# A delta-rule attention followed by an MLP mixer: elements 2 and 3 in one joint recurrence, their mixers in groups of 384 tokens with 15 block products for both channel products

## The chip, the cores and the metric

The kernel runs on one core of one Trainium2 chip. The metric is the device time of one execution in microseconds (us). Before the change it is 638.55 us, the median of three runs that lie between 637.54 and 639.22 us. The profile shown below is one further execution of the same program, and its span, from the first to the last instruction, is 636.9 us; the change is reckoned against that span, and the 1.6 us between it and the median are added at the end.

## The reference

Two blocks follow each other. The first is a delta-rule attention over batch 4, 8 heads, 768 tokens, head width 48; the second is an MLP mixer over the result, laid out as 4 elements of 768 tokens by 384 channels.

```python
k_n = k / (np.linalg.norm(k, axis=-1, keepdims=True) + 1e-06)
for t in range(S):
    y[:, :, t] = np.einsum('bhd,bhde->bhe', q[:, :, t], state)
    v_old = np.einsum('bhde,bhd->bhe', state, kt)
    state = state + bt[:, :, :, None] * np.einsum('bhd,bhe->bhde', kt, vt - v_old)
...
x = attn_out.transpose(0, 2, 1, 3).reshape(B, S, H * D)
xt = x.transpose(0, 2, 1)
h = np.maximum(xt @ w_tok1, 0.0) @ w_tok2
u = x + h.transpose(0, 2, 1)
h2 = np.maximum(u @ w_ch1, 0.0) @ w_ch2
return u + h2
```

The token product goes from 768 tokens to 256 and back, the channel product from 384 channels to 1536 and back. Everything is float32.

## The kernel before

The kernel is one stream of some 4,650 TensorE matmuls, with the other engines around them. All its parts are Python generators, called jobs. A long string, `order`, names the jobs one after the other (`m1*5` advances job m1 five times), and each advance issues the instructions up to the next `yield`. Every engine executes its own instructions strictly in the order in which that string issued them, and semaphores hold it where its data are not ready. So the string fixes the order on each engine, and not the time at which one engine passes another. A matmul of float32 stands twice in the trace, as two records; a transpose on TensorE stands once.

The recurrence is cut into chunks of 64 tokens, 12 for each batch element, 48 in all. Two chunks are a unit u of 128 tokens. For a unit, `load_kq`, `prep` and `grams` load keys and queries, norm them, turn them and form the Gram matrices; `to_parts`, `invert`, `from_parts` and `join` invert a triangular matrix for the unit (by way of DRAM from the second element on: n_dram, w_dram). `load_v` brings the values, and GpSimd scales them (L426).

`recur(t)` then makes one chunk of one element for its 8 heads, in three groups of small matmuls with a hand-over between each two: p_k from the state (L862); VectorE subtracts the values into rest (L869); p_y and p_w (L882, L886); ScalarE copies p_w into w_t (L892); p_s and p_y (L900, L901); VectorE brings the state up to date (L909), and ScalarE puts p_y into xb, the element's 768x384 block (L914). The four elements follow each other: element 3 begins when element 2 is through.

`mixer(b)` is the MLP for one element, and TensorE works on it between the groups of the recurrence of the next element; the last one, m3, has TensorE almost to itself. It is:

- the token products: 12 matmuls of 128x384 (L1060), a ReLU, 12 more (L1073) and six additions into xb on VectorE (L1077);
- then three pairs of 128-token blocks. Each pair is transposed (L1083, evicted by ScalarE at L1087), goes through the first channel product and then through the second;
- the first channel product of element 0 is plain: 36 matmuls with 256 columns (L1140). From element 1 on (`FAST = 1`) it goes by `wide_fast`: a bilinear scheme that makes a 3 by 3 by 2 block product, 18 block products when done plainly, with 15. Its weight blocks are summed once, in place over wc1, by `sum_weights` (VectorE, L973); its 11 sums of input blocks are made for every pair by `forms` (VectorE, L1001, 128x128 each). Each of the 15 products is 4 matmuls with 128 columns (L1032), evicted from PSUM by ScalarE copies (L1041) or VectorE additions (L1044) of 512 columns, with a ReLU at the end (L1048);
- the second channel product goes by a 2 by 2 scheme with 7 products instead of 8 (`product`, L1162): 42 matmuls with 192 columns for a pair, seven additions into xb (L1091), and a store.

The weights come in by `round_weights` and `round_pair`; the latter also makes the sums of w_ch2 blocks for the 7-product scheme (L299). PSUM has eight banks: two each under the tags prep and seq, three under mlp, one for filler matmuls.

What the chunks of the chain look like in the code before:

## Time and profile before

| | |
|---|---|
| device time, median of 3 runs (lowest to highest) | 638.55 us (637.54 to 639.22) |
| span of the profiled execution | 636.9 us |
| TensorE (PE) busy | 608.5 us, 96% of the span |
| VectorE (DVE) busy | 447.9 us, 70% |
| ScalarE (ACT) busy | 268.0 us, 42% |
| GpSimd (POOL) busy | 107.2 us, 17% |
| weight loads on TensorE (PEld), over and under the matmuls | 531.5 us, 83% |
| granted TensorE clock, mean | 0.976 of full speed |
| data moved by DMA | 50.27 MB, mean 79 GB/s |

How to read the profile: a row of the groups by line says line, engine, operation, the tiles written and read, shapes and count, then busy time in us, mean duration of one in ns, and idle time of the engine before them with what ended it. Matmuls are pipelined, so that the duration of one record (some 200 to 500 ns) is longer than the distance at which records follow each other; a price per matmul is taken from start to start. A row of the chain of waits says start, length and what ran; a row of the timeline says start, length and instruction, with equal neighbours merged.

### The profile page before, as it was taken

What the parts mean: (1) busy time and instruction counts of PE and PEld (TensorE: products, weight loads), DVE (VectorE), ACT (ScalarE), POOL (GpSimd) and SP (SyncE); (2) the same over time, 40 slices, a digit from 0 to 9 for tenths busy, and PEclk for the clock granted to TensorE, in tenths of its full rate; (3) what the DMA queues carried; (4) which work ended last, traced back from release to release, by engine and by line L of the source; (5) the groups of instructions that cost most, each with busy time, mean ns of one, the idle gap of its engine ahead of it and who ended that gap; (6) DMA issues with size and microseconds to landing.
All of it is one profiled execution on the core that took longest, in us unless ns stands there. A gap on an engine that the chain in (4) does not pass through costs nothing.

```text
span 636.9 us, 21542 instructions
## 1 busy us (share of the span) xinstructions
PE 608.5 (96%) x9132; PEld 531.5 (83%) x9132; DVE 447.9 (70%) x1132; ACT 268.0 (42%) x693; POOL 107.2 (17%) x146
## 2 busy tenths in 40 slices
PE   8488988899999999999999999999999999999997
PEld 5367877668898988859889999769999987999997
DVE  4987876967999658988969987776728253373643
ACT  7758785447523342215624323325334130232240
POOL 2348354235210211111111001000010000000000
PEclk9978796999999999999999999999999999999999
DMA  9686666666543355344454223202020000000000
GB/s 201 127 148 151 153 142 153 162 135 162 110 113 89 71 116 101 76 109 79 90 103 95 43 82 58 48 5 42 5 53 2 27 2 0 26 1 26 2 26 26
DMA packets 135776, 50.27 MB, mean 79 GB/s; under 512 B 114656, under 2 KB 130144, under 8 KB 135680
## 3 DMA queue, kind: packets, MB, share of 16 engines
q1 hardware_dynamic: 135680, 48.89, 35.2%
q8 instruction: 72, 1.18, 0.8%
q14 instruction: 24, 0.20, 0.1%
HBM read 39.42 MB, written 9.44 MB: 77 GB/s over the span
## 4 chain that ended last, share of the span: by engine, by line
PE 82%; DVE 7%; ACT 4%; DMA 3%; issue 2%; POOL 1%; SPq 1%; ACTq 0%; DVEq 0%; POOLq 0%
PE p_o L1162 26%; PE p_r L1032 20%; PE p_c L1140 8%; PE p_h L1073 5%; PE p L1060 4%; PE p_k L862 3%; PE p_g L453 3%; PE p_y L882 3%; PE p_s L900 3%; PE p_w L886 1%; DVE sub L681 1%; DVE x L686 1%; PE p_y L901 1%; PE p_ut L1083 1%; PE p_z L785 1%
## 5 line engine op out<-in xcount | busy, mean ns | idle before, releaser
L1162 PE MATMUL p_o<-wc,r 128*128 128x192 f32 x720 | 126.1, 329 | 0.6 <-ACT u_t L1087 0.6
L1162 PEld LDWEIGHTS p_o<-wc,r 128*128 128x128 f32 x720 | 116.8, 190 | 2.7 <-ACT u_t L1087 1.1
L1044 DVE TENSOR_TENSOR r<-r,p_r 128x512 f32<-128x512 f32 x90 | 59.8, 684 | 38.1 <-PE p_r L1032 34.3
L1091 DVE TENSOR_TENSOR xb<-xb,p_o 128x192 f32<-128x192 f32 x84 | 29.3, 350 | 57.8 <-PE p_o L1162 57.3
L1041 ACT COPY r<-p_r 128x512 f32<-128x512 f32 x54 | 31.3, 585 | 85.7 <-PE p_r L1032 76.1
L686 DVE TENSOR_TENSOR x<-x,sub 128x84 f32<-128x84 f32 (+24 forms) x178 | 59.4, 334 | 6.1
L681 DVE TENSOR_TENSOR sub<-x 128x84 f32<-128x84 f32 (+24 forms) x178 | 58.0, 326 | 6.8 <-DMA x<-n_dram 2.3
L1162 PE MATMUL p_o<-wc,s 128*128 128x192 f32 x288 | 51.5, 331 | 0.3 <-DVE xb L1091 0.3
L1140 PE MATMUL p_c<-u_t,wc 128*128 128x256 f32 x216 | 51.0, 386 | 0.2 <-ACT u_t L1087 0.2
L1162 PEld LDWEIGHTS p_o<-wc,s 128*128 128x128 f32 x288 | 46.7, 190 | 1.4 <-DVE xb L1091 0.6
L1048 ACT ACTIVATE r<-r 128x512 f32<-128x512 f32 x54 | 34.0, 631 | 26.7 <-DVE r L1044 26.2
L426 POOL TENSOR_TENSOR v_st<-v_st,nrm 128x384 f32<-128x384 f32 x24 | 20.1, 838 | 146.3 <-DMA v_st<-in_v_dram 109.3
L1140 PEld LDWEIGHTS p_c<-u_t,wc 128*128 128x128 f32 x216 | 39.7, 190 | 6.0 <-ACT u_t L1087 0.4
L516 POOL TENSOR_TENSOR mb<-mask_c,cs 128x512 f32<-128x512 f32 x20 | 21.2, 1062 | 138.9 <-DVE cs L494 138.6
L914 ACT ACTIVATE xb<-p_y 64x192 f32<-64x192 f32 x96 | 31.2, 325 | 23.6 <-PE p_y L901 12.2
L892 ACT COPY w_t<-p_w 128x192 f32<-128x192 f32 x48 | 15.2, 316 | 58.0 <-PE p_w L886 57.5
L1032 PE MATMUL p_r<-u_t,wc 128*128 128x128 f32 x288 | 38.7, 277 | 0.0
L453 PE MATMUL p_g<-kq 48*64 48x128 f32 (+1 forms) x704 | 33.6, 281 | 3.8 <-ACT kq L529 3.3
L1032 PE MATMUL p_r<-t_d,wc 128*128 128x128 f32 x288 | 37.3, 280 | 0.0
L1032 PEld LDWEIGHTS p_r<-u_t,wc 128*128 128x128 f32 x288 | 35.3, 192 | 0.4
L1060 PE MATMUL p<-xb,w 128*128 128x384 f32 x96 | 34.9, 511 | 0.0
L1032 PEld LDWEIGHTS p_r<-t_d,wc 128*128 128x128 f32 x288 | 34.0, 192 | 0.8
(184 smaller groups left out, 1212.2 us busy)
## 6 DMA issues: line engine op xcount, KB each, us to landing
d<-in_moe_w_ch_dram SPq DMA_DIRECT2D x24, 384.0 KB, 3.5
v_st<-in_v_dram SPq DMA_DIRECT2D x96, 48.0 KB, 2.7
out_dram<-xb SPq DMA_DIRECT2D x23, 192.0 KB, 1.9
kst<-in_k_dram SPq DMA_DIRECT2D x64, 48.0 KB, 2.9
n_dram<-gm SPq DMA_DIRECT2D x72, 32.0 KB, 2.4
pads<-in_k_dram SPq DMA_DIRECT2D x24, 96.0 KB, 2.9
pads<-in_q_dram SPq DMA_DIRECT2D x24, 96.0 KB, 2.9
gm<-w_dram SPq DMA_DIRECT2D x72, 32.0 KB, 2.1
```

The source lines that it names most:

```text
L453: nc.tensor.matmul(p_g[PAR[i ^ cc], p], kqt[f, p, cc, 0], kqt[f, p, cc])
L681: nc.vector.tensor_tensor(out=tmp, in0=y[:, :, 0:s, s : s + 1].to_broadcast([n, k, s, w]), in1=y[:, :, s : s + 1, s + 1 : m].to_broadcast( ...
L686: nc.vector.tensor_tensor(out=y[:, :, 0:s, s + 1 : m], in0=y[:, :, 0:s, s + 1 : m], in1=tmp, op=ALU.add,)
L914: nc.scalar.mul(y[:, :, D * i : D * i + D], p_y[PAR[1 - i]], 1.0 if c else -1.0)
L1032: nc.tensor.matmul(p[:, i], pieces[i // width][:, at : at + 128], f[f"u{n}"], start=first and i == 0, stop=True, skip_group_check=True,)
L1041: nc.scalar.copy(o, p)
L1044: nc.vector.tensor_tensor(out=o, in0=o, in1=p, op=ALU.add if sign > 0 else ALU.subtract)
L1048: nc.scalar.activation(o, o, ACTF.Relu)
L1060: nc.tensor.matmul(p_1[dh], piece_of(w1, c, 0)[:, dh * 128 : (dh + 1) * 128], xb[:, c], start=(c == 0), stop=(c == NCH - 1),)
L1073: nc.tensor.matmul(p_h, piece_of(w2, j, c * 128)[:, c * 128 : (c + 1) * 128], r1[j], start=(j == 0), stop=(j == NDH - 1),)
L1140: nc.tensor.matmul(p_c[:, k], piece_of(wc1, cb, f * 128)[:, f * 128 : (f + 1) * 128], u_t[:, cb], start=(cb == 0), stop=(cb == NCB - 1),)
L1162: nc.tensor.matmul(p, a[:, m], wc2[:, m, j], start=(start and i == 0), stop=(i == NM - 1), skip_group_check=True,)
```

## The change

It does four things.

1. Elements 0 and 1 keep their recurrences. Elements 2 and 3 run in one joint recurrence, `recur_pair(c)`: 12 steps, each with 16 heads (8 of each element) in the same three groups, and with one operation of 384 columns where two of 192 stood. Units 12 to 23 alternate between the two elements (`where`). Element 2's output goes into its xb; element 3's goes into a corner of the pads tile and from there to DRAM (x_dram), because both xb buffers are still in use, and `fetch_last` loads it back.
2. The mixer of element 1 takes the plain first channel product (as element 0's), and the second by 7 products as before.
3. The mixers of elements 2 and 3 are written anew, in four groups of 384 tokens (g = 0 to 3). `token_part` is the old token product. `first_part(g)` is the first channel product by 15 of 18 block products, 2 halves of 15 steps, each step two matmuls with 192 columns. `act_forms(g)` sums blocks of its result on GpSimd, 15 additions of 128x512. `last_part(g)` is the second channel product by the same 15-product scheme with the two operands' roles exchanged, 15 steps of four matmuls with 192 columns, each evicted by VectorE additions of 192 columns. The sums of w_ch2 blocks for it are made late, by `tail_weights` on VectorE; since the blocks that `round_pair` overwrites are needed for that, `put_aside` copies one of them for each m to DRAM (wc_dram) beforehand.
4. The string `order` is new from the first inversion (i0) on; before that it is the same.

```diff
-    nrms = tiles("nrm", [128, NP, 2], NV + 2)
+    nrm_t = const.tile([128, NV + 2, NP, 2], FP32, name="nrm")
...
-    FAST = 1
...
+    def put_aside(m):
+        assert (id(wc2), 2 * m) in rounded
+        nc.sync.dma_start(out=wc_dram[m], in_=wc2[:, m, 1])
+        put_by.add(m)
+        yield
...
+    def recur_pair(c):
...
+        heads = [
+            (e, p, i, PAR[i ^ cc], PAR[1 - i])
+            for e in range(2) for p in range(NP) for i in range(2)
+        ]
+        rest = rw_t
+        if c > 0:
+            p_k = ps_seq([128, 2, NP, D], "p_k")
+            for n, (e, p, i, r, _) in enumerate(heads):
+                f = FEATS[i]
+                nc.tensor.matmul(p_k[r, e, p], ops[e][1][f, p, cc, 0], ss_t[f, e, p])
...
+            nc.vector.tensor_tensor(out=rest, in0=p_k, in1=vsts["pair", c], op=ALU.subtract)
...
+        nc.scalar.copy(rw_t, p_w)
...
+                nc.vector.tensor_tensor(out=ss_t, in0=ss_t, in1=p_s, op=ALU.subtract)
...
+        nc.sync.dma_start(
+            out=x_dram[C * c : C * c + C].rearrange("s (i n) -> s i n", i=2),
+            in_=side[rows],
+        )
...
+    r2_of = [
+        t[:, 0:RT].rearrange("p (f n) -> p f n", f=NHT) for t in (gm_flat, kq_flat)
+    ]
...
+    def tail_weights():
+        nc.sync.dma_start(out=wc2[:, :, 1], in_=wc_dram.rearrange("m p n -> p m n"))
+        yield
+        for out, x, y, sign in SUMS_3:
+            x, y = (w_of[z] if isinstance(z, str) else wc_blocks[z] for z in (x, y))
+            nc.vector.tensor_tensor(out=w_of[out], in0=x, in1=y, op=op_of(sign))
+            yield
+        nc.vector.tensor_scalar_mul(w_of["u7"], w_of["u7"], -1.0)
+        yield
...
+    def first_part(g):
...
+        f = named(bl, late(9, [128, 4, TW], 4))
+        for n, (out, x, y, sign) in enumerate(SUMS_3):
+            x, y = (f[z] if isinstance(z, str) else bl[z] for z in (x, y))
+            nc.vector.tensor_tensor(out=f[out], in0=x, in1=y, op=op_of(sign))
+            if n % 2 == 1 or n == 10:
+                yield
+        for half in range(2):
...
+            for chain, n, reads in CHAINS:
+                first = chain not in bank
+                if first:
+                    bank[chain] = ps_mlp([128, 2, TW], "p_r")
+                p = bank[chain]
...
+                for i in range(2):
+                    q = 2 * half + i
+                    at = q % width * 128
+                    nc.tensor.matmul(
+                        p[:, i], pieces[q // width][:, at : at + 128], f[f"u{n}"],
+                        start=first and i == 0, stop=True, skip_group_check=True,
+                    )
+                yield
+                for j, e, sign, last in reads:
+                    at = FT * j + 2 * half
+                    o = r2[:, at : at + 2, TW * e : TW * e + TW]
+                    if (j, e) not in begun:
+                        nc.scalar.copy(o, p)
...
+                    else:
+                        nc.vector.tensor_tensor(out=o, in0=o, in1=p, op=op_of(sign))
+                    if last:
+                        nc.scalar.activation(o, o, ACTF.Relu)
...
+    def act_forms(g):
...
+        for out, x, y, sign in (
+            ("w12", (1, 2), (0, 2), -1), ("w3", (1, 0), (0, 0), -1),
+            ("w1", (0, 0), (1, 2), -1), ("w5", (1, 2), (2, 0), 1),
...
+        ):
+            x, y = (f[z] if isinstance(z, str) else a[z] for z in (x, y))
+            nc.gpsimd.tensor_tensor(out=f[out], in0=x, in1=y, op=op_of(sign))
+            yield
...
+    def last_part(g):
...
+            for i in range(FT):
+                nc.tensor.matmul(
+                    p, a[:, i], w[:, i // 2, i % 2],
+                    start=first and i == 0, stop=True, skip_group_check=True,
+                )
+            yield
+            for j, e, sign, last in reads:
+                cut = slice(DH * e, DH * e + DH)
+                o = xb[:, c0 + j, cut]
+                nc.vector.tensor_tensor(out=o, in0=o, in1=p, op=op_of(sign))
...
+    j23*3 r34*3 T2*2 v23*4 s r34*7 v23 m1*2 r35*4 T2 r35*3 T2
+    r33 r35*6 s*7 T2 s T2*4 A0*7 T2*3 A0*16 s*2 A0*41 l*6 A0*5 A1 T3*3 F0*4 B0 A1
+    W*11 T3*3 W*2 B0 A1*3 B0 F0*2 T3*3 B0*2 A1*20 F0*2 B0*2 F0*3 B0 A1*4 B0 F0
+    A1*24 B0*2 A1*2 B0 A1*2 B0 A1*4 B0*3 A1*8 A2 B0 A2 B0*4 T3*3 A2 B0*2 F1 A2*8
+    F0 A2*4 B0*3 A2*3 F0*2 A2*6 F1*9 B0 F1*5 B0 A2*2 B0 A2*5 B1 A2*22 B1*10 A2*4
+    B1*3 A2*3 B0 A2 B1*2 A2*4 F2 A2*4 B1*6 A3*9 B1*3 F2 B1*2 A3*8 F2*5 B2 A3*4 B2
+    A3*3 B1*2 A3*3 B2*2 A3*4 B2*3 F2*4 B2 F2*2 B2*2 F2*2 A3*22 B1 B2*3 A3*5 B2*2
+    A3*5 B2*4 A3*4 F3 A3*2 F3*4 B2*9 B3*5 F3*5 B2*2 B3*13 F3*4 B3 F3 B3*11
```

In the string, r is a step of the recurrence (r24 to r35 are the joint ones), m0 and m1 the mixers of elements 0 and 1, T2 and T3 `token_part`, A, F and B `first_part`, `act_forms` and `last_part` of a group, W `tail_weights`, s `sum_weights`, l `fetch_last`.

More of the change, by code (lines that the diff above doesn't have):

```diff
@@ L1176, in mixer @@
             if c + 2 < NCH:
-                u_t, t_c = yield from turn_pair(c + 2)
+                u_t = yield from turn_pair(c + 2)
             yield from product(p_o2, a12, 2, True)
@@ L1220 @@
         jobs[f"i{rnd}"] = invert(rnd)
-    for t in range(B * NQ):
+    for t in range(B * NQ // 2):
         jobs[f"r{t}"] = recur(t)
-    for b in range(B):
+        if t < NQ:
+            jobs[f"r{B * NQ // 2 + t}"] = recur_pair(t)
+    jobs["l"] = fetch_last()
+    for b in range(2):
         jobs[f"m{b}"] = mixer(b)
+        jobs[f"T{2 + b}"] = token_part(2 + b)
+    jobs["W"] = tail_weights()
+    for g in range(4):
+        jobs[f"A{g}"] = first_part(g)
+        jobs[f"F{g}"] = act_forms(g)
+        jobs[f"B{g}"] = last_part(g)
     pieces = [
@@ L1233 @@
         jobs[f"w{j}"] = piece
+    for m in range(NM):
+        jobs[f"q{m}"] = put_aside(m)
     jobs["s"] = sum_weights()
```

494 lines of the change are left out of this document (332 added, 162 removed), and 23 rows, old and new, of tables (CHAINS, SUMS_3, bank, w4).

## The prediction

> **What bounds the kernel now.** I read the page's engine shares and its chain of waits first, then the sums by stretches of time, then the chain in order of time for prices, then the groups by line and the timelines of single places.
>
> ```profile
> span 636.9 us, 21542 instructions
> PE 608.5 (96%) x9132; PEld 531.5 (83%) x9132; DVE 447.9 (70%) x1132; ACT 268.0 (42%) x693; POOL 107.2 (17%) x146
> ...
> PE 82%; DVE 7%; ACT 4%; DMA 3%; issue 2%; POOL 1%; SPq 1%; ACTq 0%; DVEq 0%; POOLq 0%
> ```
>
> ```profile
> 0.00:150.00 150.00, 127.52 (x2568) 98.55 (x2568) 114.46 (x302) 102.43 (x276) 62.40 (x84) 0.90 0.72 153
> 150.00:550.00 400.00, 397.95 (x5953) 351.57 (x5954) 288.82 (x729) 142.20 (x379) 44.78 (x63) 1.00 0.30 65
> 550.00:600.00 50.00, 49.41 (x374) 48.42 (x373) 30.18 (x74) 16.09 (x28) 0.00 (x0) 1.00 0.04 13
> 600.00:637.00 37.00, 33.67 (x242) 32.98 (x240) 14.42 (x29) 7.30 (x12) 0.00 (x0) 1.00 0.06 22
> ```
>
> In the second view the columns are the stretch, its length, the busy time of PE, PEld, DVE, ACT and POOL with counts, the granted clock, the DMA share and GB/s. TensorE sets the end. It idles 22.5 us in the first 150, where loads and the inversion hold it (clock 0.90), and 2.05 us in the next 400. So a matmul saved after 150 us is worth its distance to the next one, and a stall there adds in full. POOL does nothing after 550 us.
>
> **Matmul work.** The prices of the dense matmuls stand in the chain in order of time (start, length, what; two records make one matmul):
>
> ```profile
> 194.81 9.26 PE p_c L1140 x42
> ...
> 519.01 7.74 PE p L1060 x24
> ...
> 577.44 13.67 PE p_r L1032 x120
> ...
> 594.01 12.07 PE p_o L1162 x72
> ```
>
> With 256 columns: 9.26/21 = 0.441 us; with 128: 13.67/60 = 0.228; with 192: 12.07/36 = 0.335. Removed: the 15-product first part of elements 1 to 3, 9 pairs x 60 = 540 at 0.228 = 123.1, and the 7-product second part of elements 2 and 3, 6 x 42 = 252 at 0.335 = 84.4. Added: element 1's plain first part, 108 at 0.441 = 47.6; `first_part`, 4 x 60 = 240, and `last_part`, 4 x 60 = 240, all at 0.335 = 160.8. Net 208.4 - 207.5 = **+0.9 us**. Two thirds of the gain on elements 2 and 3 (5.7) is less than what element 1 pays (6.6). Token products, transposes, Gram matmuls, inversion and the number of recurrence matmuls stay.
>
> **Entries into small matmuls.** A group of small matmuls between dense ones costs more than its matmuls:
>
> ```profile
> 433.50 1.95 PE L1032 MATMUL p_r<-t_d,wc 128*128 128x128 f32 x16
> 435.29 1.06 PE L1032 MATMUL p_r<-t_c,lent 128*128 128x128 f32 x8
> 436.27 0.25 PE L882 MATMUL p_y<-s_t,kq 48*64 48x48 f32 x1
> ...
> 436.73 0.22 PE L882 MATMUL p_y<-s_t,kq 48*64 48x48 f32 x1
> 436.74 0.22 PE L886 MATMUL p_w<-rest,gm 64*64 64x48 f32 x1
> 436.88 0.45 PE L826 MATMUL p_x<-gm,zst 32*32 32x32 f32 x32
> ```
>
> Sixteen dense records take 435.29 - 433.50 = 1.79, so eight should take 0.90; the eight before the small group take 0.98: 0.08 more. Small records follow each other at 0.01, but the last one of a group is 0.14 from what comes next. An entry and exit cost some 0.22 us. After the first p_c matmul, TensorE's order enters small work 85 times in the kernel before and 49 times in the changed one, since a joint step has 3 groups where two steps had 6 (12 x 3 = 36). 36 x 0.22 = **-7.9 us**. It could be less where a group now waits for its operands; half of it, -4, is my other end.
>
> **The recurrence's hand-overs.** Between p_w and p_s lies one ScalarE copy, between p_k and p_w and between p_s and the next p_k one VectorE operation:
>
> ```profile
> L1068 ACT ACTIVATE r<-p 128x384 f32<-128x384 f32 x8 | 3.9, 490 | 14.2 <-PE p L1060 14.2
> L892 ACT COPY w_t<-p_w 128x192 f32<-128x192 f32 x48 | 15.2, 316 | 58.0 <-PE p_w L886 57.5
> L1044 DVE TENSOR_TENSOR r<-r,p_r 128x512 f32<-128x512 f32 x90 | 59.8, 684 | 38.1 <-PE p_r L1032 34.3 <-ACT gm L807 2.1 <-ACT r L1041 0.9
> L1077 DVE TENSOR_TENSOR xb<-xb,p_h 128x384 f32<-128x384 f32 x24 | 13.0, 548 | 9.0 <-PE p_h L1073 8.9
> L1087 ACT COPY u_t<-p_ut 128x384 f32<-128x384 f32 x24 | 10.4, 482 | 44.7 <-PE p_ut L1083 44.7
> ```
>
> The copy of 0.316 with TensorE's 0.22 for its last record and about 0.2 for two hand-overs needs 0.75 us of other matmuls to hide; with 384 columns (0.482) 0.9, and VectorE's 0.548 needs 1.0. Counting the work placed in each gap at the prices above: in chunks 12 to 23 the new order has ten gaps under 0.5 us where the old one has four, some +3.5; in elements 2 and 3 the 12 joint steps have four short gaps, the 24 old steps more, -1.5. VectorE also loses 24 of its 192-column operations there and all sums of input blocks, in the stretch where it was 72% busy (288.82 of 400): -4 to 0, I take -2. Together **0** (-5 to +5). In the first 150 us I keep the time, +-3: up to the first p_c matmul the two orders issue nearly the same instructions (1,204 and 1,224 matmuls).
>
> **The new tail.** From the last joint step on, TensorE has only the dense work of elements 2 and 3, some 195 us: 160.8, twice 24 token matmuls at 7.74/12 = 0.645, and transposes. Evictions of `first_part` (384 columns, 0.548) come every 0.67 us, those of before (512 columns, 0.684) every 0.91, so VectorE is a little tighter; the first token part of the tail now stands alone, with its ReLU, addition and copy (0.49, 0.548, 0.482) bare. I put **+4** on these (2 to 8).
>
> The larger term is the place of GpSimd. 60 additions of two full operands, 128x512, run on it in the tail, and VectorE's sums (`tail_weights`, `first_part`) read two SBUF operands too. What happens when both do:
>
> ```profile
> 147.17 0.36 DVE L911 COPY s_t<-p_s 128x192 f32<-128x192 f32 x1
> 147.44 2.06 DVE L299 TENSOR_TENSOR wc<-wc 128x192 f32<-128x192 f32 x2
> 149.43 0.34 DVE L869 TENSOR_TENSOR rest<-p_k,v_st 128x192 f32<-128x192 f32 x1
> ```
>
> ```profile
> 147.37 1.01 POOL L284 TENSOR_TENSOR wc<-w_f,d 128x384 uint32<-128x384 uint32 x1 [4.37 <-ACT d L278]
> 148.34 0.95 POOL L534 TENSOR_TENSOR gm<-lent,cs 128x384 f32<-128x384 f32 x1
> 149.25 1.15 POOL L516 TENSOR_TENSOR mb<-mask_c,cs 128x512 f32<-128x512 f32 x1
> ```
>
> ```profile
> L299 DVE TENSOR_TENSOR wc<-wc x24: 343/351/1158, 100.0 to 178.8; 128x192 f32<-128x192 f32 x24
> ...
> L516 POOL TENSOR_TENSOR mb<-mask_c,cs 128x512 f32<-128x512 f32 x20 | 21.2, 1062 | 138.9 <-DVE cs L494 138.6 <-DMA kst<-in_k_dram 0.2
> L534 POOL TENSOR_TENSOR gm<-kst,cs 128x384 f32<-128x384 f32 x16 | 13.4, 840 | 5.8 <-PE p_y L901 5.8
> L284 POOL TENSOR_TENSOR wc<-w_f,d 128x384 uint32<-128x384 uint32 x24 | 24.6, 1028 | 46.8 <-DVE w_f L280 18.3 <-ACT d L278 16.8 <-issue 7.6
> ...
> L973 DVE TENSOR_TENSOR wc<-wc 128x512 f32<-128x512 f32 x7 | 4.8, 687 | 0.1
> ```
>
> Two L299 sums, 0.35 us each when alone (the median), take 2.06 here: each ends about 0.2 after a GpSimd instruction ends, one per instruction. L869 at 149.43, with one operand in PSUM, takes its usual 0.34 while GpSimd runs. So a VectorE operation with two SBUF operands waits for the GpSimd one under way, and they alternate. The L534 between two sums takes 0.95, and 0.84 on average, so a sum adds 0.12 to the GpSimd instruction behind it and hides 0.23 of its own 0.35.
>
> The Trainium skill says of this pair in "SBUF — State Buffer", section "SBUF: two separate sides", that the port pair is an exclusive lock held for the whole instruction. By that L534 and one sum would take 0.84 + 0.35 = 1.19 together, and the rows say 0.95: the trace agrees on the waiting and not on the length. By the rule alone the three places below would cost some 6 us more.
>
> For `act_forms` I take GpSimd's 1.06 of the same type and size (L516; one operand broadcast); from the two full operands of L284, scaled by columns, it may be 1.3. A long sum of `tail_weights`, 768 columns, is 0.687 + 256 x 1.05 ns = 0.95 alone, and about 1.06 + 0.95 - 0.23 = 1.78 in alternation; a short one (192) 1.06 + 0.12 = 1.18.
>
> - Group 0 to 1. When `first_part(0)` ends, F0 has 12 additions ready and VectorE's queue holds the 11 sums of W, then four sums, then the additions that free the PSUM banks of the three p_h; A1's first matmul needs such a bank. TensorE has 16.5 us of T3, B0 and transposes until then. Alone the sums end in time with 2.3 us to spare; alternating they take 11 x 0.83 = 9.1 more, so TensorE stalls 6.8, and 1.8 more at its fifth step, whose bank waits behind seven more sums: **+8.6**.
> - Group 1 to 2. F1 starts 9 us before A2's 11 sums; four or five of them still meet it. 4 x 0.83 - 0.3 spare = **+3**.
> - Group 2 to 3. F2 starts only 5 us before A3's 11 sums: 11 x 0.83 - 2.1 spare = **+7**. In both cases the fifth step of the group waits, as its bank's addition stands behind all 11 sums in VectorE's queue.
>
> Together **+18.6**, with 1.3 per GpSimd addition 27, and nothing if the two keep clear of each other. GpSimd's results themselves are in time: after A3 it needs 15 x 1.06 = 16 us, and TensorE has 8 us of B2 and then takes them at 1.34 a step. The 25 added DMAs (x_dram, wc_dram and back) lie in a stretch with a DMA share of 0.30 and land before their readers.
>
> **Sum.** 636.9 + 0.9 - 7.9 + 0 + 4 + 18.6 = 652.5, and with the 1.6 us between span and median **654 us**.
>
> **Rivals.**
>
> - *GpSimd costs nothing* (faster). It is one mechanism: VectorE's sums slip between GpSimd's instructions, or F0 runs while W has not begun. It decides at the place of group 0 to 1: if W's 11 sums take no more than 13 us instead of 20, TensorE never waits. For it: the plan fits that gap with 2.3 us to spare, as if laid out so. Against it: every back-to-back GpSimd stretch in the trace blocks such sums. It gives 654 - 18.6 = 635, or 631 with VectorE's relief in the recurrence at its full 4.
> - *VectorE becomes the bound of `first_part`* (slower still). Late steps have seven additions in six steps, 3.8 us of 4.0; any wait before them isn't made up. 8 halves x 1.5 us: 654 + 12 = 666. Against: the old evictions had nearly the same ratio (0.684 to 0.91) and TensorE idled 0.6 us in 50 (550 to 600).
> - *It moves work and no time.* Half of the lock's price and half of the gain by fewer entries: 636.9 + 0.9 - 4 + 4 + 3 = 641 and the 1.6: 642.
>
> **Chances.** 0.58 for the forecast (644 to 662), 0.24 for the first rival, 0.10 for the second, 0.08 for the third. A run of this kernel is told from no change by about 0.3%, 1.9 us. Faster 0.23 (nearly all of the first rival), within 0.05 (its edge and the third's), slower 0.72. The range 632 to 667 leaves out the better half of the first rival and the worse half of the second.
>
> **What would show it.** PE idle in the last 200 us in three clumps, each at the start of a group, ended by VectorE; `tail_weights` at about 1.8 us mean and the sums of `first_part` well over 0.35; p_r and p_o matmuls both at 0.335. TensorE's small groups entered some 36 times fewer, and the tail beginning at about 435 us. I am wrong if `tail_weights` runs at 0.95, or if the loss stands in the recurrence between 150 and 435 us.

## The result and the profile after

The changed kernel takes **683.47 us**, the median of 4 runs (680.95 to 686.13), against 638.04 (637.27 to 639.22, 4 runs) for the kernel before on the same chip: a ratio of 1.070, 95% interval 1.066 to 1.075. The prediction, 654 us in a range of 632 to 667, had the sign right and the size wrong by 29.5 us. In one of the later kernels (the second with split evictions) an execution more than 1.5% above its fastest one is left out of the figures. The page of the changed kernel, its first lines, its shares in the chain of waits and GpSimd's new group:

```profile
span 683.5 us, 20751 instructions
PE 617.6 (90%) x8724; PEld 533.9 (78%) x8724; DVE 451.2 (66%) x1031; ACT 261.4 (38%) x687; POOL 192.7 (28%) x206
...
PE 48%; DVE 22%; DMA 9%; SPq 9%; issue 5%; ACT 5%; POOL 1%; DVEq 0%; ACTq 0%; POOLq 0%
...
L1337 POOL TENSOR_TENSOR gm<-gm 128x512 f32<-128x512 f32 x30 | 45.4, 1531 | 61.6 <-ACT gm L1298 60.7
```

TensorE's share of the chain falls from 82% to 48%; VectorE (7 to 22), DMAs (3 to 9) and SP's own issue time (1 to 9) take it over. The same stages of the two kernels, before first, in the view by stretches (stretch, length, busy PE, PEld, DVE, ACT, POOL, granted clock, DMA share, GB/s). The edges are the first run of p_c matmuls, the third run, and, before, the end of the recurrence; in the changed kernel the end of the small matmuls and the first p_r matmul of `first_part`:

```profile
0.00:137.60 137.60, 115.37 (x2310) 89.13 (x2310) 107.92 (x285) 93.03 (x247) 55.86 (x77) 0.89 0.72 154
137.60:229.30 91.70, 91.18 (x1640) 79.97 (x1641) 73.58 (x184) 40.75 (x120) 24.42 (x30) 1.00 0.49 109
229.30:519.00 289.70, 287.91 (x4423) 256.40 (x4422) 210.18 (x535) 107.00 (x281) 26.90 (x40) 1.00 0.28 60
519.00:636.90 117.90, 114.08 (x763) 106.02 (x761) 56.20 (x130) 27.23 (x48) 0.00 (x0) 1.00 0.04 14
```

```profile
0.00:143.00 143.00, 117.11 (x2347) 91.39 (x2347) 111.23 (x285) 95.76 (x250) 58.25 (x80) 0.88 0.69 150
143.00:243.80 100.80, 94.55 (x1606) 82.85 (x1605) 74.08 (x179) 39.96 (x118) 23.29 (x27) 0.95 0.46 103
243.80:464.00 220.20, 210.29 (x3696) 179.39 (x3696) 142.87 (x353) 69.92 (x203) 28.09 (x40) 0.98 0.36 80
464.00:476.00 12.00, 12.00 (x51) 7.11 (x48) 5.63 (x15) 3.58 (x9) 0.00 (x0) 1.00 0.53 156
476.00:683.50 207.50, 183.65 (x1036) 173.18 (x1034) 117.36 (x202) 52.17 (x107) 83.05 (x60) 0.95 0.03 12
```

Up to the third p_c run both kernels do the same matmul work, and the changed one is there 14.5 us later (243.8 against 229.3). In the stretch of the joint steps TensorE idles 220.20 - 210.29 = 9.9 us, against 1.8 in the longer stretch of before. In the tail it idles 23.9 us against 3.8, and the granted clock, 1.00 from 137 us on in the kernel before, is under 1.00 in every long stage.

To add these up I priced every matmul record of both traces at the distance at which its kind follows itself in dense runs (0.112, 0.163, 0.216 and 0.323 us for 128, 192, 256 and 384 columns; 0.013 or 0.028 for the small ones) and called the rest of the time to the next record its loss. Losses so defined hold waits, slow clock and the entries into small groups. The priced work is 528.7 us in both, and the 4.4 us before the first matmul and from the last one on are the same too.

| loss, us | before | changed | difference |
|---|---|---|---|
| start to first p_c run | 64.1 | 68.1 | +4.0 |
| first to third p_c run | 9.8 | 20.3 | +10.5 |
| to the tail (recurrence and mixers) | 27.6 | 32.7 | +5.1 |
| tail (before: from 519; changed: from 476) | 2.3 | 29.3 | +27.0 |

The sum of the differences, 46.6, is the difference of the spans. In the tail the groups of waits of the changed kernel (what waited, for whom; us in total, times, longest) show the three group changes the prediction named (the 3.6 and the 1.0 belong to one), and nothing beside them over 0.9 us:

```profile
PE p_r L1283 <- DVE kq L1296: 8.1, 1, 8.1
PE p_r L1283 <- DVE xb L1216: 7.2, 1, 7.2
PE p_r L1283 <- DVE gm L1296: 3.6, 1, 3.6
PE p_r L1283 <- DVE t_d L1266: 1.0, 1, 1.0
PE p_a L1355 <- POOL gm L1337: 0.9, 1, 0.9
```

At the first of these places (group 0 to 1) GpSimd's and VectorE's timelines stand side by side:

```profile
496.69 22.62 POOL L1337 TENSOR_TENSOR gm<-gm 128x512 f32<-128x512 f32 x12 [41.33 <-ACT gm L1298]
```

```profile
497.26 1.52 DVE L1244 TENSOR_TENSOR wc<-wc 128x768 f32<-128x768 f32 x1
498.71 2.02 DVE L1244 TENSOR_TENSOR kq<-wc 128x768 f32<-128x768 f32 x1
500.65 3.96 DVE L1244 TENSOR_TENSOR wc<-wc 128x768 f32<-128x768 f32 x2
...
518.11 1.61 DVE L1246 TENSOR_SCALAR wc<-wc 128x768 f32<-128x768 f32 x1
519.64 0.34 DVE L1363 TENSOR_TENSOR xb<-xb,p_a 128x192 f32<-128x192 f32 x1
519.91 0.88 DVE L1266 TENSOR_TENSOR t_d<-pads 128x192 f32<-128x192 f32 x3
520.82 0.36 DVE L1266 TENSOR_TENSOR t_d<-t_d,pads 128x192 f32<-128x192 f32 x1
521.10 1.01 DVE L1216 TENSOR_TENSOR xb<-xb,p_h 128x384 f32<-128x384 f32 x2
```

Twelve GpSimd additions take 22.62 us, 1.88 each, with one long VectorE sum between two of them; each sum shows as some 2.0. They run in step until 519, and only then does the addition at 521.10 free the PSUM bank that A1's first matmul (521.70) has waited for.

### The profile page after: what moved, and what is told of

It reads as the page before. It is cut to its first block, busy times and chain, and to the rows that moved or that the text cites. A ratio compares the mean times of both kernels' runs of the same rounds, so it can differ in the third digit from the quotient of the medians.

```text
span 683.5 us, 20751 instructions
## 1 busy us (share of the span) xinstructions
PE 617.6 (90%) x8724; PEld 533.9 (78%) x8724; DVE 451.2 (66%) x1031; ACT 261.4 (38%) x687; POOL 192.7 (28%) x206
## 4 chain that ended last, share of the span: by engine, by line
PE 48%; DVE 22%; DMA 9%; SPq 9%; issue 5%; ACT 5%; POOL 1%; DVEq 0%; ACTq 0%; POOLq 0%
PE p_r L1283 12%; PE p_c L1449 6%; PE p_o L1470 6%; PE p_a L1355 5%; PE p_b L1355 5%; DVE x L734 4%; DVE sub L729 4%; SPq L701 4%; DVE t_d L1266 3%; PE p_g L501 3%; DMA x<-n_dram 2%; PE p_h L1212 2%; SPq L676 2%; DVE wc L1244 2%; SPq L434 1%
## 5 line engine op out<-in xcount | busy, mean ns | idle before, releaser
L1449 PE MATMUL p_c<-u_t,wc 128*128 128x256 f32 x432 | 103.7, 393 | 0.5 <-DVE xb L1409 0.5
L1449 PEld LDWEIGHTS p_c<-u_t,wc 128*128 128x128 f32 x432 | 81.7, 194 | 13.1 <-DVE xb L1409 0.9
L1470 PE MATMUL p_o<-wc,r 128*128 128x192 f32 x360 | 65.1, 334 | 1.3 <-DVE xb L1409 1.3
L1337 POOL TENSOR_TENSOR gm<-gm 128x512 f32<-128x512 f32 x30 | 45.4, 1531 | 61.6 <-ACT gm L1298 60.7
L1470 PEld LDWEIGHTS p_o<-wc,r 128*128 128x128 f32 x360 | 59.3, 192 | 2.5 <-DVE xb L1409 1.4
L1283 PE MATMUL p_r<-t_d,wc 128*128 128x192 f32 x160 | 33.7, 349 | 11.7 <-DVE kq L1296 8.1
L507 DVE TENSOR_TENSOR gm<-p_g,mb 128x512 f32<-128x512 f32 x44 | 28.8, 684 | 14.8 <-PE p_g L501 11.5
L501 PEld LDWEIGHTS p_g<-kq 48*64 48x64 f32 (+1 forms) x704 | 30.1, 151 | 9.0 <-ACT kq L577 6.1
L1283 PE MATMUL p_r<-pads,wc 128*128 128x192 f32 x128 | 26.2, 334 | 7.2 <-DVE xb L1216 7.2
L1293 ACT COPY kq<-p_r 128x384 f32<-128x384 f32 x24 | 11.5, 478 | 48.4 <-PE p_r L1283 48.4
L390 DVE STREAM_TRANSPOSE kq<-pads 128x512 f32<-128x512 f32 x24 | 25.8, 1102 | 3.8 <-PE p_w L934 1.8
```

Of the source, the lines that this page charges most:

```text
L390: nc.vector.transpose(kq_of[p // 2][:, i, :, p % 2].rearrange("f p (s g) -> f p g s", g=G), rows_of[i].rearrange("s p (g d) -> s p g d", g ...
L501: nc.tensor.matmul(p_g[PAR[i ^ cc], p], kqt[f, p, cc, 0], kqt[f, p, cc])
L507: nc.vector.tensor_tensor(out=blocks(gm_of(u))[:, :, cc, D:GW].rearrange("s p (two n) -> s p two n", two=2), in0=p_g, in1=made[u][:, :, cc ...
L1283: nc.tensor.matmul(p[:, i], pieces[q // width][:, at : at + 128], f[f"u{n}"], start=first and i == 0, stop=True, skip_group_check=True,)
L1337: nc.gpsimd.tensor_tensor(out=f[out], in0=x, in1=y, op=op_of(sign))
L1449: nc.tensor.matmul(p_c[:, k], piece_of(wc1, cb, f * 128)[:, f * 128 : (f + 1) * 128], u_t[:, cb], start=(cb == 0), stop=(cb == NCB - 1),)
```

## The experiments

Each run stands beside runs of the kernel before on the same chip (medians 638.9 to 640.4; 638.0 on the chip of the result). The changed kernel itself was not run again there, so a difference of 2 or 3 us from its 683.47 says nothing. Losses are by the pricing above, from one profile of each run.

**1. Is the tail's loss the block between GpSimd and VectorE?** GpSimd is taken out of the tail:

```diff
-            nc.gpsimd.tensor_tensor(out=f[out], in0=x, in1=y, op=op_of(sign))
+            nc.scalar.copy(f[out], x)
```

> The 60 sums of act_forms become copies of their first operand on ScalarE (the second operand is left out), so GpSimd does nothing in the tail. In the changed kernel TensorE loses 31.6 us from the tail's first product to the end, against 2.3 in the kernel before. Theory 1 (GpSimd's two-operand instructions block VectorE's two-operand sums): the three stalls at the group changes vanish, tail_weights' long sums go from about 2.0 to 0.95 us, first_part's from 1.3 to 0.35, the granted clock stays at 1.00, the tail loses 4 to 6 us and the time is 655 to 659. Theory 2 (VectorE's queue is too full by itself: 11 to 23 sums stand ahead of the additions that free PSUM banks, whatever GpSimd does): sums at their short lengths, but the stalls of 7 and 8 us shrink by less than half and the time stays above 668.

667.38 us (667.26 to 670.88; ratio 1.044, 1.041 to 1.048). The tail's loss goes from 29.3 to 9.3 us. In the groups of this run the long sums take their length alone, and the tail is 20 us shorter at a clock of 0.99:

```profile
L1244 DVE TENSOR_TENSOR wc<-wc 128x768 f32<-128x768 f32 x6 | 5.6, 954 | 0.1
L1266 DVE TENSOR_TENSOR t_d<-pads 128x192 f32<-128x192 f32 x20 | 6.4, 352 | 2.1 <-ACT pads L1260 2.1
```

```profile
478.20:665.60 187.40, 178.32 (x1036) 169.03 (x1034) 88.80 (x202) 84.04 (x167) 0.00 (x0) 0.99 0.04 13
```

The mechanism is theory 1's; the time is 8 to 12 us above what it said. Of the 9.3 us still lost 4.3 are one wait that ends at 567.33, where ScalarE's first-write copies (L1293) now stand behind the copies that I put there, and this execution was 2.3 us late at the third p_c run. The block is not only one of sums with two operands: the scaling at 518.11 (L1246) reads a single SBUF operand, and it took 1.61 us beside GpSimd and 0.55 in this run.

**2. One place alone.** `tail_weights` ahead of F0:

```diff
-    ... m1*2 r35*4 T2 r35*3 T2 r33 r35*6 s*7 T2 s T2*4 A0*7 ...
-    ... T3*3 F0*4 B0 A1 W*11 T3*3 W*2 B0 ...
+    ... m1*2 W r35*4 T2 r35*3 T2 r33 r35*6 s*7 T2 s T2 W*4 T2*3 A0*7 ...
+    ... A0*3 W A0*4 W A0*4 W ... T3*3 F0*4 B0 A1 T3*3 B0 ...
```

> tail_weights moves ahead: its DMA right behind the last step of m1, its 11 sums and the sign change into T2 and A0, before GpSimd's F0 begins. Nothing else moves. Theory 1 (the two engines block each other): the first stall of 7.2 us (group 0 to 1) and the slow clock behind it go, the other two (3.6 and 8.1 us) stay; time 671 to 675. Theory 2 (the four-block sums of A1 meet F0 all the same and hold the banks): under 4 us, 680 or more. If the sums now delay A0's additions, some of the gain is lost inside A0: 675 to 679.

682.03 us (681.09 to 683.42), within the runs of the changed kernel and in the time of theory 2. In the trace the stall of group 0 to 1 is gone, the other two stay at 3.6 and 8.1 us, and the tail loses 23.0 instead of 29.3; but that execution had reached the third p_c run at 246.9, 3 us later than the profile of the changed kernel, by instructions that the two share. Those 3 us are the spread of this front: 241.5 to 250.6 in ten profiles of it. The 6.3 us belong to theory 1 by the trace; the medians alone don't show them.

**3. The sums on VectorE.** With the early `tail_weights`, all 60 additions of `act_forms` on VectorE, behind the sums of the next group and spread out:

```diff
-            nc.gpsimd.tensor_tensor(out=f[out], in0=x, in1=y, op=op_of(sign))
+            nc.vector.tensor_tensor(out=f[out], in0=x, in1=y, op=op_of(sign))
```

> tail_weights early as in its own run, and the 60 sums of act_forms on VectorE (0.69 us each, 41 us), set behind the sums of the next first_part and spread at one per two steps. Nothing is left out. Theory 1 (the block between the two engines is the tail's loss, and VectorE has room: 100 us busy of the last 210 in the run with ScalarE's copies): the tail loses 6 to 10 us instead of 31 and the time is 658 to 663. Theory 2 (VectorE at two thirds has its additions late behind sums): the tail loses over 14, time 667 or more.

667.63 us (664.45 to 671.8; ratio 1.045, 1.039 to 1.051). Nothing is left out, VectorE does 41 us more work, and 16 us are won; the tail loses 10.6. The tail's loss is just above theory 1's 6 to 10 us and under the 14 of theory 2; the time is in theory 2's range, 5 to 10 us above what theory 1 said. With the first experiment it shows that blocking, not VectorE's load, made the tail slow.

**4. The half-speed stretches.** In the stretches right behind the three stalls of the changed kernel, and in a quiet one for comparison:

```profile
522.20:524.70 2.50, 2.50 (x9) 2.50 (x8) 2.46 (x9) 0.48 (x1) 0.00 (x0) 0.50 0.00 0
569.30:572.40 3.10, 3.10 (x11) 3.10 (x10) 0.55 (x1) 0.48 (x1) 0.00 (x0) 0.50 0.17 63
621.90:627.00 5.10, 5.10 (x17) 5.10 (x17) 1.08 (x3) 0.96 (x2) 0.00 (x0) 0.50 0.09 33
476.00:496.00 20.00, 20.00 (x118) 18.69 (x117) 12.20 (x25) 10.14 (x21) 0.00 (x0) 1.00 0.00 1
```

TensorE is busy throughout, at a granted clock of 0.50: 17 records in 5.10 us are 0.30 each, where 0.163 is usual. So idle matmuls were set into the stalls, 8, 4 and 9 of them:

```diff
-    ... A1*20 ...
+    ... z*8 A1*20 ...   (likewise z*4 ahead of the fifth product of A2, z*9 of A3)
```

> The changed kernel with 8, 4 and 9 matmuls of 512 columns on the warm-up tile (6.9, 3.4 and 7.7 us) set where TensorE stalls for 7.4, 3.8 and 8.2 us in the tail. They add work and take no wait away. After each of these stalls the trace shows a stretch of half speed at a granted clock of 0.50 that costs 1.3, 1.6 and 2.5 us. Theory 1 (the clock is cut when TensorE picks up work after idling): the half-speed stretches vanish from the tail and the time falls by 3 to 6 us, 677 to 681. Theory 2 (they have another cause, or the stalls only shift): half-speed stretches stay in the tail, time 682 to 687.

682.86 us (682.07 to 688.57). The same places in this run:

```profile
516.68 7.03 PE L227 MATMUL p_warm<-warm 128*128 128x512 f32 x16
524.09 0.92 PE L1283 MATMUL p_r<-pads,wc 128*128 128x192 f32 x4 [0.38 <-DVE xb L1216]
...
613.48 7.89 PE L227 MATMUL p_warm<-warm 128*128 128x512 f32 x18
621.75 1.57 PE L1283 MATMUL p_r<-t_d,wc 128*128 128x192 f32 x8 [0.38 <-DVE kq L1296]
```

Eight p_r records behind the last stall take 1.57 us; in the changed kernel they took 2.93. No half-speed stretch is left in the tail, which is 4.8 us shorter (loss and filler 24.5 against 29.3) although it holds 18.1 us of added matmuls. That the stalls bring the half speed is shown by the trace of the tail; the time is the one that theory 2 gave, and no proof, since the spread of the front hides the gain. The Trainium skill has this rule in "TensorE: Matmul & The Clock Gate", section "Part 1: The HAM clock gate (the 'warmup' mystery)": the array runs at half clock after a window of about 3.4 us without work until a busy one has passed. The traces of the tail agree: half speed behind stalls of 3.6 to 8.1 us, none where they are filled.

The clock is part of the loss ahead of the tail as well, though nothing was filled there. In the changed kernel it is 0.50 from 152.7 to 156.1, from 227.8 to 234.6 and from 333.6 to 340.5 us, and TensorE's busy time in these stretches (9.2 us in the first two, 6.9 in the third) at half speed is some 4.6 us lost between the first and the third p_c run and 3.4 in the joint steps.

**5. Is the early loss the order?** The first part of the order list replaced by that of the kernel before, up to the first joint step, with the six `put_aside` steps set in late:

```diff
-    p4*2 t2*3 x t3*2 p4*2 x t3 i0*2 w13 p4*2 w18 w17*2 i0 k4 i0*3 v1 k8 i0 k6 k5 ...
+    p4*2 t2*3 x t3*2 p4*2 x t3 i0*2 w13 p4*2 w18 w17*2 i0 k4 i0*9 p4 i0*2 p4*2 c4 k8 ...
```

> The order list of the changed kernel, its first part replaced by that of the kernel before up to the first joint step (the six put_aside steps are set in just before the last step of the weight pairs they precede). Theory 1 (the new order of the early steps costs the 14.5 us by which the third run of p_c matmuls starts late, 243.8 against 229.3): the third run begins at 229 to 233 and the time is 668 to 673. Theory 2 (code, not order: the put_aside DMAs and the waits on them, or the pairing of units): the third run still begins after 239 and the time is 679 or more.

679.58 us (675.59 to 680.75). The first p_c run began at 137.3 as before the change, the third at 237.7, between the two theories, and one wait is as long as what is missing. VectorE in that run:

```profile
DVE wc L311 <- DMA wc_dram<-wc: 10.0, 2, 8.9
```

I had put a `put_aside` DMA behind eight others in SP's queue, and VectorE, whose next sum overwrites the block, waited for it with the recurrence's subtraction behind.

> As the run with the old front, with each put_aside DMA four steps behind the even weight piece that it saves. In that run VectorE waited 8.9 us for one such DMA, which stood behind eight others in SP's queue, and the third run of p_c matmuls began at 237.7. Theory 1 (the new order of the early steps costs 14.5 us, and the rest of the earlier run was this one wait): the third run begins at 229 to 232 us, time 667 to 672. Theory 2 (the put_aside waits come with the changed code wherever they stand): VectorE still waits over 4 us for them, the third run begins after 235 and the time is 676 or more.

Moved ahead, it was worse: 693.52 us (692.06 to 695.87), the first p_c run at 155.5. Now SP waited 20.5 us for GpSimd to make the pieces, with the loads of other units behind it:

```profile
SPq L296 <- POOL wc L286: 20.5, 4, 7.5
```

Six DMAs of 96 KB are nearly free to carry and cost up to 18 us by where they stand in a queue. Issued from GpSimd's queue, directly behind the instruction that makes the piece, they can block no load:

```diff
-        nc.sync.dma_start(out=wc_dram[m], in_=wc2[:, m, 1])
+        nc.gpsimd.dma_start(out=wc_dram[m], in_=wc2[:, m, 1])
```

> The changed kernel with its six put_aside DMAs issued from GpSimd's queue, right behind GpSimd's own instruction that makes the piece, instead of SP's. Order and all else unchanged. Moving these six by some steps cost 18 us in one earlier run (the first p_c matmuls at 155.5) and one wait of 8.9 us in another. Theory 1 (the six DMAs, which make SP wait for GpSimd and hold the loads behind them, are most of the early loss): the third run of p_c matmuls, at 244 to 247 in the kernels with this front, comes before 237 and the time is 671 to 676. Theory 2 (the new order itself is the loss): it stays within 3 us of 244 and the time is 680 to 686.

> The old front again, its six put_aside DMAs from GpSimd's queue, so that SP's queue holds the loads of the kernel before in their order. Theory 1 (order of the early steps plus SP's queue make the whole 14.5 us): p_c runs begin at 137 to 138, 187 to 189 and 229 to 232 as in the kernel before, time 667 to 671. Theory 2 (something else in the changed code costs there too): third run after 235, time 674 or more.

With the new order 688.67 us (685.49 to 692.86) and the third run at 246.9, no gain: there, the six DMAs in SP's queue are not the loss. With the old front 669.72 (667.43 to 674.72; ratio 1.047, 1.042 to 1.053): 13.8 us less than the changed kernel. Its second stage is that of the kernel before to 0.2 us, at full clock:

```profile
139.70:231.20 91.50, 91.06 (x1640) 79.86 (x1641) 72.80 (x181) 40.77 (x119) 25.96 (x32) 1.00 0.50 112
```

The early loss is the order's. In the changed kernel's second stage TensorE waits 2.5 us in two for operands of the inversion (p_z), 1.7 in three for ScalarE's copies after p_w, and runs at half speed as said above; with the old front two waits of 0.2 are left. Two tests of how it comes about through SP's queue failed:

> The changed kernel with the 12 stores of elements 0 and 1 (each waits for VectorE's last addition) issued from GpSimd's queue, not SP's, where they waited 20.3 us behind inversion instructions while loads stood behind them. Theory 1 (these waits in SP's queue make the operands late): the groups between 143 and 464 us lose at least 4 us less than their 20.3 + 32.1, time 676 to 679. Theory 2 (the loads behind them are early enough): within 2 us, 681 to 686; GpSimd blocked instead could make it slower, 687 to 690.

> The changed kernel with the 72 DMAs that take blocks to the inversion and the 72 that bring them back issued from GpSimd's queue, so that SP's queue is half as long between 75 and 450 us (each issue takes SP 0.45 us; bursts of 8 to 12 of them stand in the chain of waits). Theory 1 (SP's issue time is what the new early order runs into): the third run of p_c matmuls, 244 to 247, begins before 240 and the time is 670 to 678. Theory 2 (order of VectorE's work and operands decides, SP's length does not): within 3 us of 244, time 680 to 686. GpSimd's own work behind the 144 issues could make it slower: above 690.

The stores from GpSimd's queue: 685.17 us (682.60 to 686.99), losses within 0.4 of the changed kernel's in each stage. Loads behind a waiting store were early enough. The blocks from GpSimd's queue: 699.28 (698.18 to 700.94), third run at 258.5; each issue kept GpSimd 0.59 us. That shows neither that SP's issue time matters nor that it doesn't. Which instruction of the new order costs the most is open, and so is whether the inversion in VectorE's queue, tested below for its last three rounds alone, does the same here.

**6. The joint steps.** First the width of the evictions:

```diff
-            nc.vector.tensor_tensor(out=rest, in0=p_k, in1=vsts["pair", c], op=ALU.subtract)
+                    nc.vector.tensor_tensor(
+                        out=rest[:, e], in0=p_k[:, e], in1=vsts["pair", c][:, e],
+                        op=ALU.subtract,
+                    )
```

> In a joint step VectorE's subtraction after p_k and the one after p_s are made in two halves of 192 columns, each as soon as its element's matmuls are issued; ScalarE's copy stays whole. From 244 to 452 us the groups of small matmuls hold about 15.7 us of waits in the changed kernel (5.4 in the kernel before, 229 to 519). Theory 1 (the 384-column evictions are late): the waits fall by 3 to 6 us, time 677 to 681. Theory 2 (the order leaves too little work between hand-overs or the operands come late by other ways): within 1.5 us of the changed kernel, 682 to 685, or slower by the 22 added instructions' fixed time.

> In the first split run VectorE's first half stood ahead of the scaling of the values that it subtracts and waited for their loads, so it told nothing. Here a half is issued early only where the scaled values are there, else both halves come where the whole one stood. Theory 1 (the 384-column evictions are late): the waits of 15.7 us in the joint steps fall by 3 to 6, time 677 to 681. Theory 2 (VectorE's queue or the operands make them late, not the width): within 2 us of the changed kernel, 681.5 to 686.

716.61 us (713.51 to 723.35) and 705.27 (702.63 to 709.44). The first run's groups of waits say why; the second's has the same 13.0 in ten, and 8.4 in ten for p_k:

```profile
PE p_s L1033 <- DVE ss_t L1044: 13.0, 10, 2.8
PE p_k L995 <- DVE rw_t L998: 10.3, 11, 3.0
```

Both halves lie in one PSUM tile, and TensorE's matmuls for the second half waited for VectorE to have read the first: one hand-over had become two. That refutes neither theory; half-width evictions would need tiles of their own, which wasn't tried. Then VectorE's queue:

```diff
             w = m - 1 - s
+            if rnd >= 4:
+                yield
+                continue
```

> The row steps of the inversion are left out for its last three rounds (units 14 to 23), so about 84 VectorE instructions of 0.3 to 0.8 us are gone between 250 and 450 us; the loads, stores and joins around them stay. Theory 1 (the joint steps' hand-overs wait because VectorE's queue is full with the inversion): the waits between 244 and 452 us fall by 8 or more, time 671 to 676. Theory 2 (the list of steps leaves too little work between one hand-over and the next): they fall by less than 4, time 679 to 684.

> The kernel before with the same row steps of the inversion left out (last three rounds), as a control: in the changed kernel this took 11.7 us of waits (32.1 to 20.4) out of the stretch of the joint steps. Theory 1 (joint steps make TensorE wait on VectorE's queue where the single steps did not): here it takes less than 5 us out of 229 to 519 us (27.6 us beyond the dense matmul prices), time 633 to 638. Theory 2 (any recurrence waits as much on the inversion): 8 us or more, time 627 to 631.

In the changed kernel 677.66 us (674.46 to 679.92; ratio 1.059, 1.055 to 1.063): the stretch of the joint steps loses 20.4 instead of 32.1 us, and TensorE idles 208.00 - 205.66 = 2.3 there instead of 9.9, at full clock:

```profile
251.00:459.00 208.00, 205.66 (x3691) 176.05 (x3691) 84.98 (x173) 69.39 (x203) 27.61 (x40) 1.00 0.39 84
```

The median is 1.7 us above what theory 1 said; this execution, the slowest of the four, was 6.8 us late at the third p_c run (250.6). In the kernel before, the same cut changes nothing: 638.27 (636.68 to 641.13, 10 runs), ratio 1.000 (0.998 to 1.002), 27.8 us against 27.6. So the inversion's row steps cost the new recurrence some 8 to 12 us and the old one nothing, although VectorE is the less busy one now (142.87 of 220.20 against 210.18 of 289.70). 11.7 is the upper end: 3.4 of it is the half-speed stretch at 333.6, which the profile of the new order with the `put_aside` DMAs on GpSimd's queue does not have; with the same instructions its stretch is 216.9 us long, not 220.2. Without these steps the new kernel loses 21.0 us from the third p_c run to the tail and the old one 27.8, and the 6.8 between them are about what the fewer entries into small groups were priced at. TensorE's longest waits in the changed kernel's stretch:

```profile
PE p_k L995 <- DVE ss_t L1043: 2.1, 1, 2.1
PE p_z L833 <- DVE t L803: 1.5, 2, 0.9
...
PE p_o L1470 <- DVE xb L1409: 1.3, 1, 1.3
```

Of 9.9 us, 2.8 are for VectorE's evictions of the joint steps (the 2.1, and 0.7 for L1001), 2.3 for operands of the inversion itself (p_z, on two of VectorE's operations) and 1.8 for its additions in the mixer; 1.5, ahead of a p_s, have no cause in the profile. The chain of waits at the longest one:

```profile
416.62 0.47 DVE r L1429
417.09 0.32 DVE sub L729
417.43 0.41 DVE x L734
417.86 0.41 DVE sub L729
418.29 0.40 DVE x L734
418.69 0.48 DVE ss_t L1043
419.17 0.04 issue
419.21 0.84 PE p_k L995 x21
```

The step's addition (L1043) came in VectorE's queue behind sums and inversion steps, and the next p_k waited 2.1 us for it. Last, these steps were spread evenly, in the changed kernel and in one with all that had helped:

```diff
-    ... m1*2 r27 m1*7 k22*2 i5*3 k22 i5*3 k22 i5 p22 i5 p22 r29 ...
+    ... m1 i5 m1 i5 r27 i5 m1 i5 m1 i5 m1 i5 m1 i5 m1 i5 m1 i5*2 m1 ...
```

> The changed kernel with the steps of the inversion's last three rounds spread evenly between their first and last place (one per step of the mixer) instead of runs of 3 to 9; nothing else moves and nothing is left out. Leaving these steps out took the stretch of the joint steps from 32.1 us beyond the matmul prices to 20.4, and the control on the kernel before took nothing. Theory 1 (the joint steps' evictions stand behind runs of these steps in VectorE's queue): the stretch falls to 24 to 28 us, time 676 to 680. Theory 2 (VectorE's total work there, not its place, makes them late): 30 to 34, time 681 to 686.

> The same spreading in the kernel with the old front, the early tail_weights and act_forms' sums on VectorE, which took 651.5. Theory 1: 3 to 7 us off, 645 to 649, which still leaves it behind the kernel before. Theory 2: 650 to 653.

686.51 us (682.85 to 687.53) and 655.10 (654.28 to 656.67): theory 1 is refuted as far as these runs of steps go, with 32.2 us against 32.1, and the second is 3.6 us slower than the same kernel without the spreading (651.47, below). The 2.1 us stall of L1043 went, and the inversion's results came later instead:

```profile
PE p_z L833 <- DVE t L803: 2.9, 2, 2.5
```

That the inversion's row steps make the waits is shown. Whether they do so by standing ahead of the evictions or by bringing their own results late is not separated, since leaving them out ends both, and both kinds stand in the waits above. A place for them that costs nothing was not found.

**7. Together.** The old front with the DMAs of `put_aside` on GpSimd's queue, the early `tail_weights` and the sums on VectorE:

> Old front with the put_aside DMAs from GpSimd's queue, tail_weights early, and act_forms' sums on VectorE: the two largest losses undone together. If they are separate terms, 14.5 and 16 us come off the changed kernel's 683.5: 652 to 656, still slower than the kernel before, by about the waits in the joint steps and the first joint-step entries. If one gives back what the other gains (another wait takes its place): above 660.

651.47 us (649.51 to 652.18; ratio 1.018, 1.014 to 1.022), 32.0 off the changed kernel: the 13.8 of the front and the 15.8 of the tail add up, with 2.4 more. Its losses by stage are 62.9, 9.6, 31.1 and 10.6: against the kernel before 8.3 us more in the tail, 3.5 more in the joint stretch and 1.4 less at the front, which is nearly all of the 11 us between them. No version beat the kernel before.

## Why the prediction was right or wrong

**The tail: right in place and mechanism.** GpSimd and VectorE block each other at the three group changes, ended by VectorE, as forecast with 8.6, 3 and 7 us; the waits are 7.2, 4.6 (3.6 and 1.0) and 8.1. The durations were a little low: a GpSimd addition takes 1.27 us alone, not 1.06 (1.3 was the other end that I kept), a pair with a long sum 1.88 instead of 1.78. The Trainium skill's rule ("SBUF — State Buffer", section "SBUF: two separate sides") of a lock for whole instructions would make that pair 1.27 + 0.95 = 2.22; here too the measurement is shorter. Stalls and new evictions were put at 22.6 us; the tail's loss grew by 27.0, of which 5.3 (1.3, 1.6 and 2.5 at the three places) are **half-speed stretches behind the stalls**, a term the sum did not have. With the 4.6 and 3.4 ahead of the tail, which no run tested, it is some 13 of the 46.6 us. It was there to see: the clock of 0.90 in the first 150 us stood in the first view, and I put it down to loads and the inversion without asking what a new stall of 7 us would do to the clock.

**Entries into small matmuls: the price right, the net wrong.** After the first p_c run TensorE enters small work 49 times instead of 85, as counted (28 of the 36 in the stretch of the joint steps; the other 8 ahead of it, where no step is joint). A lone group of a single step, before, and one of a joint step, after, each from its first small record to the next dense one:

```profile
441.73 0.25 PE L882 MATMUL p_y<-s_t,kq 48*64 48x48 f32 x1
...
442.34 0.94 PE L1032 MATMUL p_r<-t_d,wc 128*128 128x128 f32 x6
```

```profile
411.86 0.25 PE L1012 MATMUL p_y<-ss_t,kq 48*64 48x48 f32 x1
...
412.94 0.92 PE L1449 MATMUL p_c<-u_t,wc 128*128 128x256 f32 x3
```

Two single groups take 2 x 0.61, the joint one 1.08: 0.14 less, and the 0.08 ahead of a group come on top, 0.22 as priced. So the saving is there, some 28 x 0.22 = 6 us in this stretch. But its loss grew by 5.1.

**The recurrence's hand-overs: the step that failed in the middle.** I took them at 0 (-5 to +5), by counting the dense work in each gap and crediting VectorE with less work. Of this 0, +3.5 stood for chunks 12 to 23 and -3.5 for the joint steps; the stretch of the joint steps lost about 11 (5.1 and the 6 saved) instead. The count assumed that an eviction starts when its matmuls end, and had no term for the inversion. The waits stand at the hand-overs only in part (2.8 to 4.3 us of 9.9); the short-inverse runs show that the inversion's row steps on VectorE are behind 8 to 12 us, and that a fall of VectorE's mean load from 73% to 65% says nothing of that.

**The first 244 us: the other step that failed.** For the first 150 us I kept the time, +-3, as the two orders "issue nearly the same instructions"; it was +4.0 up to the first p_c run. The +3.5 of chunks 12 to 23, which run from there to the third p_c run and a little beyond, stood against 10.5. Same instructions, another order: 14.5 us together, and the old front gave them back; by which waits is known only in part. The sentence that the 25 added DMAs "land before their readers" held in the changed kernel but for 0.9 us (VectorE's L311 on wc_dram); set into the old order, six of them cost 9 to 18 us by where they stood.

**Matmul work** was put at +0.9 and is 0.0 in the priced records. The tail began, with T2's first matmul, at 452 us where 435 was forecast: that the loss would stand in the recurrence between 150 and 435 us was one of the two signs of being wrong, and 15.6 of the 46.6 us (10.5 and 5.1) do stand between 143 and 464. The misses add up: 11.0 in the front (14.5 against +3.5), 16.5 in the recurrence (+5.1 against -7.9 and -3.5), 4.4 in the tail (27.0 against 22.6), less 0.9 of matmul work, are the 31.0 us by which the span's forecast (652.5) fell short of 683.5.

**The rivals.** "GpSimd costs nothing" is out by the first experiment. "VectorE becomes the bound of `first_part`" is out by the third: with 41 us more on VectorE the tail got 19 us shorter (3.4 us of waits for the additions of `first_part` are left in it). "Moves work and no time" is out.

## What to carry to other kernels

A new order of the same instructions is an edit of its own, to be priced by the waits of each queue; where that can't be done, its range belongs in the sum, not a zero. A stall of some microseconds on TensorE costs a sixth to two fifths more than its length (1.3 us behind 7.2, 1.6 behind 3.6, 2.5 behind 8.1 in the tail), because the clock behind it is halved for 2.5 to 5 us. Fewer and larger hand-overs save their entries only if the evicting engine's queue is free when they come; and sums between SBUF tiles on VectorE shouldn't be planned beside such sums on GpSimd.

## What the hardware showed that I had not expected

Half-speed stretches followed not only the stalls of 7 and 8 us: in the run with the sums on VectorE a wait of 1.9 us (to 562.1), with one of 0.5 us shortly ahead of it (to 558.0), was followed by 3.4 us at half speed as well (563.3 to 566.7), although that is shorter than the window in the rule cited above; the wait of 2.1 us at 419.2 in the changed kernel was followed by none. And with an eviction split inside one PSUM tile TensorE waited for VectorE's read of the first half up to 2.8 us before it wrote the second; whether the chip asks for that wait or only the semaphores that the program was given, the traces don't say.
